# Keys times values in three strips of 32 columns instead of one block of 96

## The chip, the cores and the metric

The kernel runs on one core of a Trainium2 chip. The metric is the device time of one execution in microseconds (us). The core has five engines with their own instruction queues: TensorE (PE for its matmuls, PEld for its weight loads), VectorE (DVE), ScalarE (ACT), GpSimd (POOL) and SyncE (SP), which issues most of the DMAs.

## The reference

Three stages run one after the other: a gated linear attention with a complex decay, a dense gated layer, and a layer of eight experts of which each token visits one.

```python
for t in range(S):                        # batch 4, heads H = 8, S = 768, D = 48
    S_re, S_im = ar*S_re - ai*S_im + kv[t], ar*S_im + ai*S_re    # kv = outer(k[t], v[t])
    y[t] = q[t] @ S_re                                     # a_re, a_im normalised to |a| <= 0.999
x = y as (3072 tokens, 384)
x = ((x @ w_a) * (x @ w_b)) @ w_out       # w_a, w_b: 384x1536, w_out: 1536x384
e = argmax(x @ w_gate); out = softmax weight of e * (relu(x @ w1[e]) @ w2[e])   # 8 experts, 384 -> 1024 -> 384
```

## The kernel before

The 3072 tokens are worked on in twelve blocks of 256 tokens (j), three to a batch entry, and each block in two chunks (c) of 128 tokens. For the attention, the recurrence is turned into matrix products within a chunk plus a state that is carried from chunk to chunk. A head has 48 complex key channels, held as 96 rows (48 real, 48 imaginary parts). VectorE, ScalarE and GpSimd prepare the decays and phases of a block (`pre`), and DMAs bring keys and queries into the layout `kT`, `qT` (96 rows, heads, tokens).

For a chunk TensorE then does, in the function `attn`:

- `sc` (line 1209): keys times queries, four heads at a time, 128x128 scores each; VectorE masks them into `sm`.
- `kn` (line 1218): transposes of the keys, 128 tokens by 96 channels for each head; ScalarE copies them into `KN` (line 1223, tile `kn`).
- `y` (line 1248): the outputs. The 384 output channels are 12 pieces of 32 columns, and four pieces are worked on side by side: each matmul has a stationary operand of 32 columns (of `v`, or of the state `T`) and writes one of the four strips of 32 PSUM partitions. The moving operands are 128 columns wide.
- `kv` (line 1267): keys times values for the state. For each of the 8 heads one matmul, the stationary operand `KN` of 128 tokens by 96 channels, the moving operand `v` of 128 tokens by 48 columns, the result 96x48. VectorE adds it to the state (line 1273 or 1275, tile `T`) and fades it.

The last chunk of a batch entry needs no state after it, so `kv` is called 20 times: 24 chunks less four. All these operands are plain float32. Each such matmul stands in the trace as two weight loads and two matmuls (two passes): 8 matmuls of `kv` are 16 records.

The dense layer of a block follows: `up` (line 852, tile `ab_p`, 128x256 moving; for the first block line 859, in plain float32), gating on ScalarE, VectorE and GpSimd (`g`, `gH`, `gL`, lines 869 to 880), and `down` (line 889, tile `o`, moving 128x392). These use float32 split into a high and a low part, one pass each. The logits lead to a routing step (`rk`, line 587, bf16), and the experts run at the end (lines 710 and 728).

The order on each engine is set before the kernel is built, by a planner: every step is given to it with an engine, an estimated weight, what it reads and writes, and the time at which it is due (`P.add`), and the planner lays the steps of all blocks down engine by engine. So attention steps of block j stand between `up` and `down` steps of block j-1. The weight of `kv` in that plan, 1.36, is the same before and after. TensorE works through its queue in that order.

Of the kernel before, what the change touches and what calls it, by code (L numbers as in the profile page):

```python
# [15 lines left out]
H, D, C, BT = 8, 48, 128, 256  # L16
# [393 lines left out]
def fast(tc, q, k, v, a_re, a_im, w_a, w_b, w_out, w_gate, w1, w2, out, dram, x2d):  # L410

    nc = tc.nc
# [3 lines left out]
    with ExitStack() as mctx, ExitStack() as ctx:  # L416
# [424 lines left out]
        xT, ld, PT, KN, pq, made = {}, {}, {}, {}, {}, {}  # L841
# [349 lines left out]
        def attn(j, t0, t1):  # L1191
# [7 lines left out]
            for c in range(2):  # L1199
# [64 lines left out]
                def kv(c=c, S=S):  # L1264
                    t = S["kv"] = p_sc.tile([96, H, D], F32, tag="sc", name="kv_p")
                    for h in range(H):
                        nc.tensor.matmul(out=t[:, h], lhsT=KN[j, c][:, h], rhs=ld["v", j, c][:, h, 0:D], start=True, stop=True)

                def sum_(c=c, S=S, first=first):
                    T = tpad[(2 * j + c) % 2]  # L1270
# [29 lines left out]
                if not last:  # L1300
                    add("PE", 1.36, kv, [("kn", 0), ("kn", 1), v_], [("kv_p", j, c)], take="sc")
                    add("DVE", on("DVE", 384), sum_, [("kv_p", j, c), T_] + qk, [To_], give=True, alone=False)
                    add("DVE", 0.01 if first else on("DVE", 384), fade, [To_] + qk, [To_])
# [52 lines left out]
        for j in range(1, NB):  # L1356
# [14 lines left out]
            t = P.add("PE", 0.2, count, r=["oh", "acc"], w=["rk_p"], at=at + 2, take="sc")  # L1371
# [6 lines left out]
            if j == NB - 1:  # L1378
                P.add("DVE", 0.5, spanned, r=[("span", i, n) for i in range(3 * NF) for n in range(2)], w=["fit"], at=lo + 46)
                t = P.add("PE", 0.06, counted, r=["acc"], w=["so_p"], at=lo + 24, take="sc")  # L1380
# [77 lines left out]
```

## Time and profile before

| what | value |
|---|---|
| median of 3 timed runs | 944.06 us (941.37 to 945.06) |
| the profiled execution | 935.16 us |
| span of the profiled execution | 933.3 us |
| mean granted TensorE clock in it | 0.991 |
| TensorE matmul / weight load busy | 93% / 90% of the span |
| VectorE / ScalarE / GpSimd busy | 65% / 48% / 31% |
| `kv`: matmul records | 320, mean 247 ns each, 30.1 us busy |

The durations of matmuls overlap, since a matmul is started while the one before is still on its way through the array, and the end that the profile gives is modelled. What a matmul costs in a row of matmuls is therefore read from the distance between two starts, never from the duration. A timeline row gives the start of the first of a run of like instructions, the time from that start to the end of the last, and their number; the start of one row less the start of the row before it is what the earlier row cost TensorE.

### The profile page before, as it was taken

How to read it: one execution, taken by the hardware profiler on the slowest of the kernel's cores; microseconds unless marked ns; L12 is line 12 of the kernel's file. 1: busy time of each engine (PE TensorE's matmuls, PEld its weight loads, DVE VectorE, ACT ScalarE, POOL GpSimd, SP SyncE). 2: the span in 40 equal slices, each digit the busy share in tenths (PEclk: the TensorE clock that was granted, in tenths of full speed). 3: DMA queues.
4: the chain of work that ended last, by engine and by line, in shares of the span. 5: the costliest groups of instructions: out<-in, count | busy, mean ns of one | idle time of the engine just before them, and what ended most of it. 6: DMA issues, size and time to landing. Idle time of an engine off the chain costs nothing. (4 is left out here: it accounts for less than half of the span.)

```text
span 933.3 us, 18743 instructions
## 1 busy us (share of the span) xinstructions
PE 871.8 (93%) x7308; PEld 840.8 (90%) x7308; DVE 606.6 (65%) x1261; ACT 446.4 (48%) x821; POOL 288.8 (31%) x285
## 2 busy tenths in 40 slices
PE   0399899999999999999999999999999999999993
PEld 0387789899999999999999999999999999999993
DVE  7799989978676768595949496435652644545530
ACT  6453566666557354554645453224532543434430
POOL 3100002153253334352334333222235451433211
PEclk9999999999999999999999999999999999999997
DMA  9394521531625452716272715112433643454501
GB/s 250 98 337 133 178 52 50 155 112 35 162 44 162 102 154 60 213 44 195 62 194 44 212 28 153 35 52 69 139 117 114 178 143 102 147 165 131 161 23 24
DMA packets 128895, 112.69 MB, mean 121 GB/s; under 512 B 36564, under 2 KB 123446, under 8 KB 128796
## 3 DMA queue, kind: packets, MB, share of 16 engines
q1 hardware_dynamic: 122620, 101.30, 38.4%
q0 software_dynamic: 6176, 10.08, 3.8%
q8 instruction: 60, 0.98, 0.5%
q14 instruction: 39, 0.32, 0.1%
HBM read 82.42 MB, written 10.56 MB: 100 GB/s over the span
## 5 line engine op out<-in xcount | busy, mean ns | idle before, releaser
L852 PE MATMUL ab_p<-xH,wa 128*128 128x256 f32 x792 | 168.3, 289 | 0.7 <-ACT xH L1259 0.7
L852 PE MATMUL ab_p<-xH,wb 128*128 128x256 f32 x792 | 162.6, 282 | 0.0
L880 POOL TENSOR_TENSOR gL<-g,gH 128x256 fp32r<-128x256 f32 x108 | 94.8, 878 | 218.6 <-ACT gH L876 206.0
L869 ACT COPY g<-ab_p 128x256 f32<-128x256 f32 x144 | 53.5, 372 | 190.9 <-PE ab_p L852 168.9
L889 PE MATMUL o<-wo,gH 128*128 128x392 f32 x528 | 139.7, 345 | 0.0
L852 PEld LDWEIGHTS ab_p<-xH,wa 128*128 128x128 f32 x792 | 131.4, 189 | 3.1 <-issue 2.1
L852 PEld LDWEIGHTS ab_p<-xH,wb 128*128 128x128 f32 x792 | 131.7, 190 | 0.0
L872 DVE TENSOR_TENSOR g<-g,ab_p 128x256 f32<-128x256 f32 x144 | 59.9, 416 | 104.6 <-ACT g L869 104.4
L852 PE MATMUL ab_p<-xL,wa 128*128 128x256 f32 x396 | 111.5, 282 | 1.2 <-DVE xL L1262 1.2
L852 PE MATMUL ab_p<-xL,wb 128*128 128x256 f32 x396 | 111.6, 282 | 0.0
L715 DVE SCALAR_TENSOR_TENSOR hL<-h_p,hH 128x256 fp32r<-128x256 f32 (+5 forms) x80 | 41.4, 517 | 90.9 <-ACT hH L714 90.6
L714 ACT ACTIVATE hH<-h_p 128x256 fp32r<-128x256 f32 (+5 forms) x80 | 36.8, 460 | 111.7 <-PE h_p L710 110.8
L889 PE MATMUL o<-wo,gL 128*128 128x392 f32 x264 | 90.1, 341 | 0.0
L889 PEld LDWEIGHTS o<-wo,gH 128*128 128x128 f32 x528 | 89.2, 189 | 0.6 <-issue 0.4
L728 PE MATMUL o<-w2H,hH 128*128 128x384 f32 (+4 forms) x232 | 79.0, 341 | 0.0
L728 PE MATMUL o<-w2H,hL 128*128 128x384 f32 (+4 forms) x232 | 78.4, 338 | 0.0
L728 PE MATMUL o<-w2L,hH 128*128 128x384 f32 (+4 forms) x232 | 78.3, 337 | 0.0
L710 PE MATMUL h_p<-sH,w1H 128*128 128x256 f32 (+5 forms) x240 | 77.4, 322 | 0.0
L710 PE MATMUL h_p<-sH,w1L 128*128 128x256 f32 (+5 forms) x240 | 76.9, 320 | 0.0
L710 PE MATMUL h_p<-sL,w1H 128*128 128x256 f32 (+5 forms) x240 | 76.8, 320 | 0.0
L852 PEld LDWEIGHTS ab_p<-xL,wa 128*128 128x128 f32 x396 | 75.1, 190 | 1.8 <-DVE xL L1262 1.6
L876 ACT ACTIVATE gH<-g 128x256 fp32r<-128x256 f32 x132 | 54.6, 413 | 44.2 <-DVE g L872 44.0
(193 smaller groups left out, 1943.8 us busy)
## 6 DMA issues: line engine op xcount, KB each, us to landing
raw<-in_moe_w_dram SPq DMA_DIRECT2D x64, 384.0 KB, 3.8
q<-in_q_dram SPq DMA_DIRECT2D x24, 192.0 KB, 4.3
v<-in_v_dram SPq DMA_DIRECT2D x24, 192.0 KB, 3.7
raw<-in_moe_w_a_dram SPq DMA_DIRECT2D x12, 384.0 KB, 6.2
raw<-in_moe_w_b_dram SPq DMA_DIRECT2D x12, 384.0 KB, 6.7
raw<-in_moe_w_out_dram SPq DMA_DIRECT2D x12, 384.0 KB, 7.1
x2d<-x SPq DMA_DIRECT2D x24, 192.0 KB, 2.2
ck<-in_moe_w_a_dram SPq DMA_DIRECT2D x12, 384.0 KB, 3.7
```

The costliest lines, as they stand in the source:

```text
L710: nc.tensor.matmul(out=t, lhsT=lh[:, o:o + 128], rhs=rh[:, kk].rearrange("p c t -> p (c t)"), start=n == 0, stop=n == 8)
L714: nc.scalar.activation(out=hH, in_=t, func=ACTF.Relu)
L715: nc.vector.scalar_tensor_tensor(out=hL, in0=t, scalar=0.0, in1=hH.bitcast(F32), op0=ALU.max, op1=ALU.subtract)
L728: nc.tensor.matmul(out=G["o", c], lhsT=lh[:, c * r:(c + 1) * r], rhs=rh, start=f == 0 and n == 0, stop=f == NH - 1 and n == 2)
L852: nc.tensor.matmul(out=t[:, i], lhsT=lh[:, kk * 128:(kk + 1) * 128], rhs=rh[:, kk], start=n == 0, stop=n == 8)
L869: nc.scalar.copy(out=G["g", j, f], in_=G["ab", j, f][:, 0])
L872: nc.vector.tensor_tensor(out=G["g", j, f], in0=G["g", j, f], in1=G["ab", j, f][:, 1], op=ALU.mult)
L876: nc.scalar.activation(out=G["H", j, f], in_=G["g", j, f], func=ACTF.Copy)
L880: eng.tensor_tensor(out=G["L", j, f], in0=G["g", j, f], in1=G["H", j, f].bitcast(F32), op=ALU.subtract)
L889: nc.tensor.matmul(out=G["o", j, c], lhsT=lh[:, c * C:(c + 1) * C], rhs=rh, start=f == first and n == 0, stop=f == last and n == 2)
```

## The change

The loop over heads in `kv` gets an inner loop: instead of one matmul with 96 stationary columns, three matmuls with 32 stationary columns each, which write partitions 0 to 31, 32 to 63 and 64 to 95 of the same PSUM tile. The moving operand, 48 columns of `v`, is the same for the three.

```diff
                 def kv(c=c, S=S):
                     t = S["kv"] = p_sc.tile([96, H, D], F32, tag="sc", name="kv_p")
                     for h in range(H):
-                        nc.tensor.matmul(out=t[:, h], lhsT=KN[j, c][:, h], rhs=ld["v", j, c][:, h, 0:D], start=True, stop=True)
+                        for s in range(3):
+                            nc.tensor.matmul(out=t[s * 32:s * 32 + 32, h], lhsT=KN[j, c][:, h, s * 32:s * 32 + 32], rhs=ld["v", j, c][:, h, 0:D], start=True, stop=True)
```

No other instruction changes and none changes its place, on any engine. On TensorE each of the 20 rows of `kv` is replaced where it stands. Two kinds of place matter. In the first `kv` stands right behind `y`, whose stationary operands have 32 columns too; this is the difference of before and after on TensorE at the second call (a row is line, operation, tile written and operands, output partitions x columns, and count; the numbers are buffer numbers):

```order
 L1248 MATMUL y_p<-sm,v_131 32x128 x4
 L1248 MATMUL y_p<-qT,T_133 32x128 x4
-L1267 MATMUL kv_p<-v_131,kn 96x48 x8
+L1268 MATMUL kv_p<-v_131,kn 32x48 x24
 L803 MATMUL wt_p<-ident,raw 128x128 x3
 L859 MATMUL ab_p<-x,raw 128x256 x6
```

Eight matmuls have become 24, between the same neighbours. Seven of the 20 calls stand right behind `y`; one of the seven is followed by `rk`, the others by matmuls with 128 stationary columns. In the second kind of place `kv` stands between matmuls with 128 stationary columns. TensorE before, at one such call, in the middle of the kernel:

```order
L889 MATMUL o_4620<-wo_969,gL 128x392
L889 MATMUL o_4624<-wo_969,gH 128x392 x2
L889 MATMUL o_4624<-wo_969,gL 128x392
L1267 MATMUL kv_p<-v_130,kn 96x48 x8
L852 MATMUL ab_p<-xH,wa_1532 128x256
L852 MATMUL ab_p<-xL,wa_1532 128x256
```

and the same place after the change:

```order
L889 MATMUL o_4812<-wo_1001,gL 128x392
L889 MATMUL o_4816<-wo_1001,gH 128x392 x2
L889 MATMUL o_4816<-wo_1001,gL 128x392
L1268 MATMUL kv_p<-v_130,kn 32x48 x24
L852 MATMUL ab_p<-xH,wa_1596 128x256
L852 MATMUL ab_p<-xL,wa_1596 128x256
```

Only the row of `kv` differs (and buffer numbers). There are thirteen such calls: twelve behind `o` (eight with `ab` next, four with `rk` next) and the very first call, which stands behind `sc` and before `wt`.

## Rows read from the trace of the kernel before

**Rows 1.** The page: span, and busy time of the engines.
```profile
span 933.3 us, 18743 instructions
PE 871.8 (93%) x7308; PEld 840.8 (90%) x7308; DVE 606.6 (65%) x1261; ACT 446.4 (48%) x821; POOL 288.8 (31%) x285
```

**Rows 2.** Busy time by stage; columns as the first line names them.
```profile
core 0: us, PE busy (x) PEld busy (x) DVE busy (x) ACT busy (x) POOL busy (x), PEclk, DMA share, GB/s
60.00:110.00 50.00, 48.24 (x229) 39.04 (x229) 48.57 (x110) 21.77 (x46) 0.00 (x0) 1.00 0.70 217
110.00:130.00 20.00, 18.04 (x237) 16.32 (x236) 18.00 (x37) 15.02 (x28) 0.00 (x0) 0.91 0.17 41
...
260.00:420.00 160.00, 160.00 (x1590) 156.75 (x1590) 117.89 (x242) 86.17 (x155) 65.84 (x56) 1.00 0.42 113
420.00:610.00 190.00, 190.00 (x1828) 186.40 (x1826) 124.95 (x276) 87.31 (x166) 63.10 (x71) 1.00 0.43 114
```

**Rows 3.** Instructions of line 1267 (kv): count, ns min/median/max, first and last start.
```profile
L1267 PEld LDWEIGHTS kv_p<-v,kn x320: 159/165/165, 47.9 to 606.6; 128*96 128x96 f32 x160
L1267 PE MATMUL kv_p<-v,kn x320: 203/248/283, 48.1 to 606.7; 128*96 128x48 f32 x160
```

**Rows 4.** TensorE timeline, kv between o and ab: start, us, instructions.
```profile
308.31 0.34 PE L889 MATMUL o<-wo,gL 128*128 128x392 f32 x1
308.49 1.48 PE L1267 MATMUL kv_p<-v,kn 128*96 128x48 f32 x16
309.79 0.36 PE L852 MATMUL ab_p<-xH,wa 128*128 128x256 f32 x1
```

**Rows 5.** TensorE timeline, from ab into y, then kv and rk.
```profile
254.47 0.28 PE L852 MATMUL ab_p<-xL,wb 128*128 128x256 f32 x1
254.58 0.28 PE L852 MATMUL ab_p<-xH,wb 128*128 128x256 f32 x1
254.79 0.43 PE L1248 MATMUL y_p<-sm,v 128*32 128x128 f32 x8
255.03 0.41 PE L1248 MATMUL y_p<-qT,T 96*32 96x128 f32 x8
...
256.14 0.40 PE L1248 MATMUL y_p<-sm,v 128*32 128x128 f32 x8
256.36 0.40 PE L1248 MATMUL y_p<-qT,T 96*32 96x128 f32 x8
256.69 1.56 PE L1267 MATMUL kv_p<-v,kn 128*96 128x48 f32 x16
258.09 0.17 PE L587 MATMUL rk_p<-oh,strict 128*128 128x8 bf16 x1
258.12 0.17 PE L587 MATMUL rk_p<-acc,ones 128*128 128x8 bf16 x1
258.14 0.17 PE L587 MATMUL rk_p<-oh,strict 128*128 128x8 bf16 x1
```

**Rows 6.** TensorE timeline, from y out to ab.
```profile
322.95 0.40 PE L1248 MATMUL y_p<-qT,T 96*32 96x128 f32 x8
323.28 0.39 PE L852 MATMUL ab_p<-xH,wa 128*128 128x256 f32 x1
323.50 0.28 PE L852 MATMUL ab_p<-xL,wa 128*128 128x256 f32 x1
323.62 0.40 PE L852 MATMUL ab_p<-xH,wa 128*128 128x256 f32 x2
```

**Rows 7.** TensorE timeline, from y out to rk.
```profile
601.66 0.40 PE L1248 MATMUL y_p<-qT,T 96*32 96x128 f32 x8
602.00 0.18 PE L587 MATMUL rk_p<-oh,strict 128*128 128x8 bf16 x1
602.04 0.17 PE L587 MATMUL rk_p<-acc,ones 128*128 128x8 bf16 x1
```

**Rows 8.** TensorE timeline, a run of plain float32 matmuls with 256 moving columns.
```profile
57.04 2.76 PE L859 MATMUL ab_p<-x,raw 128*128 128x256 f32 x12
59.63 0.28 PE L812 MATMUL wg_p<-wg,wt 128*128 128x8 f32 x2
```

**Rows 9.** Weight loads that started in the first 70 ns of a y.
```profile
53.33 0.16 PEld L1248 LDWEIGHTS y_p<-sm,v 128*32 128x32 f32 x8
```

**Rows 10.** Records of kv by stage; columns us, PE busy (x), PEld busy (x), clock, DMA.
```profile
40.00:60.00 20.00, 3.04 (x32) 2.90 (x32) 1.00 0.89 270
110.00:130.00 20.00, 3.12 (x32) 2.87 (x32) 0.91 0.17 41
172.00:215.00 43.00, 1.56 (x16) 1.43 (x16) 0.96 0.40 114
215.00:260.00 45.00, 4.67 (x48) 4.30 (x48) 1.00 0.35 90
260.00:420.00 160.00, 7.39 (x80) 7.56 (x80) 1.00 0.42 113
420.00:610.00 190.00, 10.35 (x112) 10.59 (x112) 1.00 0.43 114
```

**Rows 11.** What TensorE waited for: us in total, times, longest.
```profile
PE kn_p L1218 <- DVE sm L1213: 1.7, 1, 1.7
PE ab_p L852 <- DVE xL L1262: 1.2, 2, 0.9
PE rk_p L587 <- DVE oh L565: 0.5, 1, 0.5
```

## The prediction

> **What bounds the kernel now.** I read the page first for the busy shares: TensorE has matmuls in flight for 93% of the span, VectorE is at 65%, the others below [rows 1]. Then the busy time by stage, since a share over the whole span says little: from 260 to 610 us TensorE is busy for every microsecond of 350, VectorE for 243 [rows 2]. There the end moves with what TensorE is given to do. From 60 to 110 us VectorE is busy 48.57 of 50 us, so time saved on TensorE ahead of that stretch would mostly be spent waiting. Third, what TensorE waits for: apart from the start-up there are a few waits, one of 1.7 us for VectorE's masks and small ones for `xL` and the routing [rows 11]. Last the timeline, for what a piece of work costs from start to start.
>
> The 20 calls of `kv` stand in the trace as 320 passes [rows 3]. By stage there are two calls before 60 us, two from 110 to 130, one from 172 to 215, then 3, 5 and 7, which makes 15 after 215 us [rows 10].
>
> **What kv costs now.** Between `o` and `ab` it takes 309.79 - 308.49 = 1.30 us, 81 ns a pass [rows 4]. Is that the moving operand? Plain float32 with 256 moving columns takes (59.63 - 57.04) / 12 = 216 ns a pass [rows 8], so 48 columns would be 40 ns in proportion. So a pass of `kv` waits for the load of its 96 stationary columns, about 0.85 ns a column; 32 columns then take about 27 ns. Behind `y` the call takes 258.09 - 256.69 = 1.40 us [rows 5].
>
> **What a strip costs.** The trace shows an operation of this kind: `y` has 32 stationary columns and writes four strips in turn. Eight of its passes start every 0.22 us [rows 5], which is two rounds of four strips at 0.11 us a round. One strip's 128 moving columns alone take half of 216, 108 ns. So the four strips run at the same time, and the load of the next 32 columns (27 ns) is hidden under the matmul. Loads of different strips also run together: the first eight passes of `y` take 255.03 - 254.79 = 0.24 us instead of 0.22, one load of 27 ns for all and not four in turn; and eight weight loads start within 70 ns of its beginning [rows 9].
>
> By this, the new `kv` is 16 rounds (8 heads, two passes) of three strips side by side, each round as long as 48 moving columns. That lies between 40 ns (in proportion) and 44 ns (110 less 80 columns at 0.83 ns, the slope between y's 110 and 216). I take 44, for y's rounds hold the overheads that these will: 16 x 44 = 0.70 us. The bounds of a round are 27 ns from below (a load alone, if the matmul were hidden under it) and 81 to 85 ns from above (three loads of 27 ns one after another, and a few ns between them); I keep to the row of `y`, the only one of this kind.
>
> **What turning the array over costs.** Going into strips and out of them isn't free, and `y` shows both. In: the last `ab` before `y` takes 254.79 - 254.58 = 0.21 us where its neighbour takes 0.11, so 0.10, and 0.02 for the slower first rounds. Out: y's last eight start at 322.95, `ab` at 323.28, 0.33 instead of 0.22, and the first `ab` takes 0.22 where the next takes 0.12, since its weights are not loaded ahead: 0.11 + 0.10 [rows 6]. With `rk` behind it, 602.00 - 601.66 = 0.34 and then 0.04 instead of about 0.03: 0.12 + 0.01 [rows 7]. So there and back costs 0.33 us, or 0.25 with `rk` next. Before the change a `kv` behind `y` paid the way out itself (256.69 - 256.36 = 0.33); it now follows in place at 0.22 and pays the way out at its own end.
>
> **The sum on TensorE.**
> - behind `o` or `sc`, `ab` or `wt` next, 9 calls: 1.30 - (0.70 + 0.33) = 0.27 us each, 2.4
> - behind `o`, `rk` next, 4 calls: 1.30 - (0.70 + 0.25) = 0.35, 1.4
> - behind `y`, six calls: (0.33 + 1.40) - (0.22 + 0.70 + 0.21) = 0.60, 3.6
> - behind `y`, `rk` next, one call: 1.73 - (0.22 + 0.70 + 0.13) = 0.68, 0.7
>
> Together 8.1 us. The 15 calls after 215 us (8 of the first kind, 4, 2 and 1) hold 2.2 + 1.4 + 1.2 + 0.7 = 5.5, and there TensorE has no idle time that could swallow it. The first two calls (0.9) stand ahead of the stretch in which VectorE is full: I count nothing. The three between 110 and 215 us hold 1.8; TensorE waits for masks, `xL` and the routing near them [rows 11], so half, 0.9. That makes 6.4 us, between 4.5 (some of the rest meets waits too) and 8.1. The profiled execution took 935.16 us and would take 928.8. The timed runs had a median of 944.06, 9 us above it; I take the same 6.4 us off and forecast 937.6 us, faster by 0.7%.
>
> What else the edit touches: a call issues 16 more matmuls, 32 more passes, whose issue is inside the rounds (the first rival prices it if it isn't). The order on the other engines stays, so nothing is moved past a queue and no wait is added. VectorE's sum waits for the last pass of `kv` and gets it earlier.
>
> **A rule against it.** Passes of `y` average 27.5 ns apart, and nothing in a long row in this trace is denser; `rk` with 8 moving columns has 20 to 30 ns between starts [rows 5]. The Trainium skill, TensorE: Matmul & The Clock Gate, section "Wait — 56ns, not 53.3ns?", says that starts of matmuls are never nearer than about 25 ns, however few columns move. By that rule 48 passes would take 48 x 25 = 1.20 us and the change would lose. In the trace eight loads and their first matmuls start within 70 ns [rows 9], so it is no limit between strips in a burst; whether it is one on the average, no row shows, since y's rounds would be 110 ns anyway.
>
> The same page (section "The mechanism") lets a weight load overlap a matmul in flight only if they use different rows of the array. All strips here use all rows, so a round would be 27 + 44 = 71 ns. The trace speaks against it: y's rounds take 110 ns with 108 of moving, so loads were hidden there.
>
> **Rivals.** The gain of 8.1 us is spread over 20 x 16 = 320 rounds, 25 ns each: the change breaks even on TensorE at about 69 ns a round. All rivals on TensorE are told by that number.
>
> - *Issue bounds it* (13%). If passes can't start nearer than 25 to 27.5 ns on the average, a round is 75 to 82 ns, 31 to 38 above mine. In the 15 late calls that is 240 rounds: 5.5 - 7.4 to 5.5 - 9.1, so 2 to 4 us lost: 946 to 948. For it: nothing denser in a row. Against it: the bursts in `y`.
> - *Strips take turns* (10%), the slower side. If the three loads go one after the other the round is 85 ns: 5.5 - 240 x 0.041, 4.3 us lost, 948. If the matmuls take turns too, 48 passes of 44 ns, a round is 131 ns: 5.5 - 240 x 0.087 = 15 us lost and 3 more in the early calls: 962. Loads that are not hidden (71 ns) would end near no change, 945. For it: three strips that read the same moving columns at once occur nowhere in the trace. It decides from 69 ns a round on. Against it: y's 0.24 and 0.22 us.
> - *TensorE gains and another engine takes it back* (15%). Then the `kv` rows shorten as forecast, but `up` or `down` waits for gating or masks; 0 to 4 us gained, 942. For it: VectorE is at 74% from 260 to 420 us. Against it: TensorE has no idle time there at all, so the others are ahead by more than the few tenths that a call saves.
>
> The forecast case holds the other 62%, with a range of its own from 934 to 940.5.
>
> **How the numbers follow.** A measurement of this kernel can tell about 0.5%, 4.7 us, from no change. The forecast's 6.4 us lies not far beyond that: of its 62%, 47 count as faster and 15 as no change. The issue case is mostly within 0.5% (10, and 3 slower), taking turns mostly slower (8, and 2 within), the third within (15). That makes faster 0.47, same 0.42, slower 0.11. The range reaches down to 933 (rounds somewhat shorter and the early calls counted), and up to 947 to take in the third case and most of the issue case.
>
> **What would show it.** In the new profile `kv` stands as 960 passes. Right: from its first start to that of the `ab` behind it about 1.03 us where it was 1.30; behind `y` it starts 0.22 us after y's last eight and not 0.33; the first `ab` or `o` behind it is slower by 0.10; the last `ab` or `o` ahead of it as well; TensorE still busy throughout 260 to 610 us, and the stretch of the dense blocks shorter by 5 to 6 us. Wrong: a `kv` of 1.2 us or more inside (issue or turns), new waits of TensorE for `g`, `sm` or `xL` (the third case), or a lower granted clock in the stretches around the calls.

## The result and the profile after

The changed kernel took 934.37 us (median of four runs, 931.75 to 935.85), the kernel before 944.56 us in the same set: a ratio of 0.9904, 95% interval 0.9881 to 0.9927. That ratio is worth 9.1 us. In a second set, with more runs, it was 927.78 against 935.83 us, 0.9912 (0.9894 to 0.9930), which is 8.2 us by the ratio. Forecast were 6.4 us, 0.9932.

There are two profiles of the changed kernel, from these two sets. Where the lines agree the second is shown. First the page, span and busy time of the engines, which answer to [rows 1]:

```profile
span 925.7 us, 20023 instructions
PE 862.1 (93%) x7948; PEld 827.8 (89%) x7948; DVE 605.8 (65%) x1261; ACT 446.1 (48%) x821; POOL 293.6 (32%) x285
```

TensorE has 640 records more of each kind and is busy for less time; its share of the span has not moved. The instructions of line 1268, which is the new `kv` [rows 3]:

```profile
L1268 PEld LDWEIGHTS kv_p<-v,kn x960: 106/110/112, 49.2 to 599.4; 128*32 128x32 f32 x192
L1268 PE MATMUL kv_p<-v,kn x960: 203/206/231, 49.2 to 599.4; 128*32 128x48 f32 x192
```

320 passes have become 960, and the last starts at 599.4 us instead of 606.7. Busy time by stage, columns as in [rows 2]:

```profile
260.00:420.00 160.00, 160.00 (x1802) 154.87 (x1801) 119.42 (x244) 85.41 (x155) 64.53 (x57) 1.00 0.43 115
420.00:610.00 190.00, 190.00 (x2037) 184.54 (x2036) 124.96 (x282) 88.06 (x167) 64.99 (x72) 1.00 0.42 111
```

TensorE is still busy for all of the 350 us, at the full clock, so what it was spared there has reached the end. The call between `o` and `ab`, the same as in [rows 4], on the timeline of TensorE:

```profile
305.31 0.34 PE L889 MATMUL o<-wo,gH 128*128 128x392 f32 x1
305.49 0.34 PE L889 MATMUL o<-wo,gL 128*128 128x392 f32 x1
305.76 0.88 PE L1268 MATMUL kv_p<-v,kn 128*32 128x48 f32 x48
306.57 0.38 PE L852 MATMUL ab_p<-xH,wa 128*128 128x256 f32 x1
306.80 0.28 PE L852 MATMUL ab_p<-xL,wa 128*128 128x256 f32 x1
```

From its own first start to that of the next instruction `kv` takes 0.81 us where it took 1.30. The `o` ahead of it takes 0.27 instead of 0.18: the way into strips. The `ab` behind it takes 0.23, since its weights are not loaded ahead. And a call behind `y` with `rk` next, the one of [rows 5]:

```profile
254.54 0.40 PE L1248 MATMUL y_p<-qT,T 96*32 96x128 f32 x8
254.76 0.86 PE L1268 MATMUL kv_p<-v,kn 128*32 128x48 f32 x48
255.55 0.18 PE L587 MATMUL rk_p<-oh,strict 128*128 128x8 bf16 x1
255.59 0.17 PE L587 MATMUL rk_p<-acc,ones 128*128 128x8 bf16 x1
```

It starts 0.22 us after y's last eight passes instead of 0.33, and takes 0.79 where it took 1.40.

The first of the two profiles shows something else. Its span is 932.9 us, hardly below the 933.3 before. There the first matmul of the experts stands 7.7 us earlier than before, and TensorE is 7.7 us ahead still at 700 us; then, on its timeline:

```profile
701.95 0.28 PE L710 MATMUL h_p<-sL,w1H 128*128 128x256 f32 x1
702.06 0.28 PE L710 MATMUL h_p<-sH,w1L 128*128 128x256 f32 x1
705.60 0.39 PE L710 MATMUL h_p<-sH,w1H 128*128 128x256 f32 x1 [3.26 <-issue]
```

It stood still for more than 3 us with nothing named that it waited for. By stage (columns as in [rows 2]):

```profile
700.00:705.00 5.00, 2.34 (x20) 2.14 (x18) 0.62 (x1) 0.88 (x2) 3.90 (x4) 1.00 0.38 103
705.00:710.00 5.00, 3.66 (x16) 3.16 (x16) 0.85 (x2) 0.47 (x2) 3.91 (x4) 0.65 0.14 36
```

VectorE and ScalarE do little, and after the pause the granted clock falls to 0.65 on the mean, part of the time at the lower level. By 715 us all 7.7 us are gone. Read against the first profile of the kernel before, which had no such pause, the change would seem to bring 0.4 us of span. The first experiments ask whether this belongs to the change.

### The profile page after: what moved, and what is told of

The parts are those of the page before. It is cut to its first block, busy times and chain, and to the rows that moved or that the text cites. A ratio compares the mean times of both kernels' runs of the same rounds, so it can differ in the third digit from the quotient of the medians.

```text
span 932.9 us, 20023 instructions
## 1 busy us (share of the span) xinstructions
PE 865.6 (93%) x7948; PEld 829.9 (89%) x7948; DVE 606.7 (65%) x1261; ACT 446.6 (48%) x821; POOL 288.5 (31%) x285
```

## The experiments

Theory: three strips run side by side, a round is as long as its moving columns, going into strips and out costs a fixed turn, and TensorE hands the saved time on because it has no idle time. Rivals: the issue of passes or the loads bound a round; the late pause belongs to the strips and eats the gain; the time comes from somewhere else.

### Both kernels again

The kernel before, unchanged.

> The kernel before, unchanged, with a second profile of its own. In the first pair of profiles the changed kernel was 7.7 us ahead at 607 us and 0.4 us ahead at the end, since TensorE stood still around 702 us in the dense run of the experts; the timed runs say 9 us in all. Theory A (stalls of that kind come and go between executions in both kernels): this execution is at or above 941 us and shows idle TensorE or a lower clock after 660 us that the first profile of before did not show; up to 607 us it agrees with that profile within 0.5 us. Theory B (the strips cause the late stall): no such stall here, about 935 us in the profile.

It took 935.93 us (ratio to itself in the set 1.0003, 0.9989 to 1.0017) and showed no pause. What theory A forecast for this run, 941 us or more and an idle TensorE, did not come: the pause is not shown in the kernel before, and theory A stands on the next run alone.

The changed kernel, unchanged.

> The changed kernel, unchanged, with a second profile. Both theories: the last kv stands 7.5 to 8 us earlier than in the kernel before. Theory A: no stall at 702 us this time, or one at another place, with 930 to 935 us and a ratio of 0.988 to 0.993. Theory B: the same stall of 3.5 us at the same place again.

927.78 us, ratio 0.9912, and no pause: from 700 to 800 us

```profile
700.00:800.00 100.00, 100.00 (x616) 96.82 (x615) 48.20 (x75) 40.80 (x75) 47.98 (x42) 1.00 0.47 138
```

TensorE is busy throughout. The weight loads of the experts (count, ns, first and last start), in the kernel before of the same set and in this run:

```profile
L710 PEld LDWEIGHTS h_p<-sH,w1H x240: 186/188/193, 671.8 to 908.3; 128*128 128x128 f32 x120
L710 PEld LDWEIGHTS h_p<-sH,w1H x240: 186/188/193, 664.4 to 900.8; 128*128 128x128 f32 x120
```

The first is 7.4 us ahead, the last 7.5. So the changed kernel is 7.4 us ahead before the experts start, the experts keep it, and theory B falls as it was put (the same pause at the same place again): none of the six profiles of kernels with strips in this second round of runs has such a pause among the experts. That strips bring one now and then is not ruled out by one profile with a pause and six without. Nor do the times settle it: both kernels took longer in the first set than in the second (8.7 and 6.6 us by the medians), and the first profile of the kernel before, 935.16 us, lies below all four timed runs of that set; whether pauses stood in those runs no profile shows. What the pause was stays open. What counts for reading is that the end of one profile can hide a gain that the same profile shows at every earlier mark.

### Another order of the same matmuls

```diff
-                    for h in range(H):
-                        for s in range(3):
+                    for s in range(3):
+                        for h in range(H):
```

> The same 24 matmuls a call in another order: the strip is the outer loop and the head the inner one, so that eight matmuls of one strip stand behind one another in the queue before the next strip comes. If strips run side by side only when neighbours in the queue use different strips, a call takes about 48 x 44 ns = 2.1 us instead of 0.70, and the kernel is 20 x 1.4 = 28 us slower than the changed one, some 20 us slower than before. Rival (each strip has a queue of its own that looks far ahead): a call stays near 0.7 to 1.0 us and the time within 3 us of the changed kernel.

945.57 us, ratio 1.0104 (1.0082 to 1.0126): slower than before, 17.8 us slower than the changed kernel. The same kind of call on the timeline:

```profile
310.49 0.34 PE L889 MATMUL o<-wo,gL 128*128 128x392 f32 x1
310.76 1.95 PE L1268 MATMUL kv_p<-v,kn 128*32 128x48 f32 x48
312.64 0.38 PE L852 MATMUL ab_p<-xH,wa 128*128 128x256 f32 x1
```

1.88 us against 0.81 for the same 48 passes. How many passes were in flight in 0.2 us at the beginning of a call (line 1268; columns us, PE busy (x), PEld busy (x), clock, DMA), strip by strip first:

```profile
310.80:311.00 0.20, 0.20 (x5) 0.20 (x6) 1.00 0.00 0
311.00:311.20 0.20, 0.20 (x9) 0.20 (x7) 1.00 0.11 3
```

and in the changed kernel:

```profile
305.80:306.00 0.20, 0.20 (x16) 0.20 (x18) 1.00 0.00 0
306.00:306.20 0.20, 0.20 (x28) 0.20 (x21) 1.00 0.11 3
```

Three times as many. So neighbours in the queue must use different strips. The call is still somewhat shorter than 48 passes one by one (48 x 42 ns is 2.0 us, and the way out comes on top). The single starts in the trace lie 42 or 43 ns apart, except for a few shorter distances (6 to 37 ns) around each of the two changes of strip. That fits a TensorE that begins the next strip while a few passes of the old one are still to come; the records don't name the strip, so this reading is not shown. My 28 us were too many for that (1.07 us a call, not 1.4), and because the early calls are partly hidden: the fifteen calls after 215 us cost 15.9 us against the changed kernel, the five ahead of it 0.8.

### What bounds a round

Strips with 64 moving columns, of which 16 are padding that nothing reads (the tile for the result is made wider to hold them):

```diff
-                            nc.tensor.matmul(out=t[s * 32:s * 32 + 32, h], ..., rhs=ld["v", j, c][:, h, 0:D], start=True, stop=True)
+                            nc.tensor.matmul(out=t[s * 32:s * 32 + 32, h], ..., rhs=ld["v", j, c][:, h], start=True, stop=True)
```

> Three strips as in the changed kernel, but 64 moving columns instead of 48: the 16 padding columns of v behind each head move too, and what they give is not read. If the moving columns set the length of a round (about 0.83 ns a column, and 42 ns at 48), a round takes 56 ns and 16 rounds 0.22 us more a call; if the issue of passes sets it, a round stays at 42 ns.

```profile
308.12 1.09 PE L1269 MATMUL kv_p<-v,kn 128*32 128x64 f32 x48
309.14 0.39 PE L852 MATMUL ab_p<-xH,wa 128*128 128x256 f32 x1
```

1.02 us against 0.81, 0.21 more: 13 ns a round for 16 columns, 0.83 ns a column (rounds of 42.5 and 55.8 ns by the single starts). The one execution took 931.66 us. The moving columns set the round.

The kernel before with 64 moving columns:

> The kernel before with 64 moving columns instead of 48, 96 stationary columns as they were. If a pass of kv waited for the load of its weights there, the pass stays at 81 to 85 ns and the call at 1.30 us; if it waited for the moving columns, it grows by a third.

```profile
308.60 1.49 PE L1268 MATMUL kv_p<-v,kn 128*96 128x64 f32 x16
309.90 0.36 PE L852 MATMUL ab_p<-xH,wa 128*128 128x256 f32 x1
```

1.30 us, as with 48 columns, and 935.36 us in the one execution. A third more to move costs nothing there: the pass waited for the load of its 96 columns.

The 48 columns in two halves, each with loads of its own:

```diff
                     for h in range(H):
-                        for s in range(3):
-                            nc.tensor.matmul(out=t[s * 32:s * 32 + 32, h], ..., rhs=ld["v", j, c][:, h, 0:D], start=True, stop=True)
+                        for d in range(0, D, 24):
+                            for s in range(3):
+                                nc.tensor.matmul(out=t[s * 32:s * 32 + 32, h, d:d + 24], ..., rhs=ld["v", j, c][:, h, d:d + 24], start=True, stop=True)
```

> Three strips, and the 48 moving columns in two halves of 24, each with its own weight loads: 48 matmuls and 96 passes a call, 32 rounds. A round is then no longer bounded by the moving columns (20 ns). Loads side by side would bound it at 27 to 30 ns, 0.9 to 1.0 us for the 32 rounds; an issue limit of 25 ns between any two passes, the first rival of the prediction, would make 75 ns a round and 2.4 us a call.

```profile
313.18 1.21 PE L1269 MATMUL kv_p<-v,kn 128*32 128x24 f32 x96
314.32 0.38 PE L852 MATMUL ab_p<-xH,wa 128*128 128x256 f32 x1
```

96 passes in 1.14 us, of which 0.12 lie between the last start and the `ab` (single starts in the trace): 1.02 us over 32 rounds is 32 ns a round and 11 ns a pass. That rules out 25 ns between starts on the average, and three loads one after another (81 ns a round). The kernel as a whole took 938.04 us in the one execution. Against the second profile of the kernel before it was 3.3 us behind at 130 us, 4.3 at 265 and 3.5 at 615: what it lost it lost ahead of 265 us, and the late calls won 0.8 back. Within two calls TensorE waited for nothing the profile names:

```profile
PE kv_p L1269 <- issue: 2.6, 2, 2.1
58.78 0.28 PE L1269 MATMUL kv_p<-v,kn 128*32 128x24 f32 x8 [2.10 <-issue]
262.54 0.18 PE L1269 MATMUL kv_p<-v,kn 128*32 128x24 f32 x1 [0.54 <-issue]
```

The first line gives the total in us, the times and the longest; the other two, from the timeline, the places. Why it waited there wasn't tried.

### The price of the turn

`kv` joined to `y` in the plan, so that it always stands right behind it. Its own step goes, its weight in the plan falls from 1.36 to 0.8, and `y` now waits for `kn` too, so the planner may order other steps anew (operands that stay are cut to `...`):

```diff
-                add("PE", 1.0 if first else 1.9, y, [("sm", 0), ...] + qk, ["y"])
+                y_r = [("sm", 0), ...] + qk
+                if last:
+                    add("PE", 1.0 if first else 1.9, y, y_r, ["y"])
+                else:
+                    add("PE", 0.8 + (1.0 if first else 1.9), lambda y=y, kv=kv: (y(), kv()), y_r + [("kn", 0), ("kn", 1)], ["y", ("kv_p", j, c)], take="sc")
 ...
-                    add("PE", 1.36, kv, [("kn", 0), ("kn", 1), v_], [("kv_p", j, c)], take="sc")
```

> Strips kept, and kv always given to the planner as one step with y, so that it stands right behind y in all 20 calls and not in 7. If the turn into strips and back costs 0.33 us (0.25 with rk next), 13 calls save one turn each: 4.0 us less than the changed kernel up to 607 us, ratio to the kernel before about 0.987. Rival (a turn is cheap, the shorter kv comes from the rounds alone): no difference from the changed kernel beyond 1 us.

923.20 us, ratio 0.9856 (0.9835 to 0.9877), 4.6 us below the changed kernel. In place it looks like this:

```profile
303.49 0.40 PE L1248 MATMUL y_p<-qT,T 96*32 96x128 f32 x8
303.71 0.86 PE L1268 MATMUL kv_p<-v,kn 128*32 128x48 f32 x48
304.51 0.18 PE L587 MATMUL rk_p<-oh,strict 128*128 128x8 bf16 x1
```

0.22 us after `y`, no turn. The profiled execution was the longest of its four (925.80 us): the first expert load stands at 662.6 us, 1.8 us ahead of the changed kernel; but between 185 and 615 us alone it gained 4.1 us on it (the same matmuls of `up`, counted through, 2.4 us behind at the first mark and 1.7 ahead at the second), 3.7 of them after 265 us. It had fallen behind early, by 4.4 us at 140 us: from 110 to 130 us the plan came out in another order and TensorE's granted clock was 0.83 on the mean (1.00 in the second profile of the changed kernel), part of the time at the lower level:

```profile
110.00:130.00 20.00, 17.62 (x294) 16.08 (x292) 15.20 (x33) 14.26 (x27) 0.00 (x0) 0.83 0.11 22
```

So the two were parted: joined from block 4 on only.

```diff
+                joined = not last and j >= 4
```

> Strips, and kv joined to y in the plan from block 4 on; the first seven calls are planned as in the changed kernel. With kv joined everywhere the plan of the stretch around 110 to 133 us came out worse (TensorE 4.9 us late there and about 2.4 us lost for good against the changed kernel), while the twelve late calls gained 4.1 us. If both parts are rightly read, this version keeps the 4.0 us of the late turns and loses nothing early: 4 us less than the changed kernel, ratio to the kernel before 0.986 to 0.988, and in the trace 4 us ahead of the changed kernel at the last up of the dense layer. Rival (the gain of the joined kernel came from a better order elsewhere): no more than 1.5 us below the changed kernel.

922.21 us, ratio 0.9868 (0.9850 to 0.9885) in a later set; the first expert load stands at 659.0 us, 5.4 us ahead of the changed kernel's second profile and 12.8 ahead of that of the kernel before. About 3.5 us of the 5.4 come after 265 us, where the late turns are. Of the rest 1.4 us come from 185 to 190 us, and not from the plan: the same 54 matmuls of `up` stand there in the same order, but the granted clock was 0.72 in the changed kernel and 1.00 here (changed kernel first, columns as in [rows 2]):

```profile
185.00:190.00 5.00, 5.00 (x34) 5.00 (x34) 3.63 (x6) 0.84 (x3) 1.89 (x2) 0.72 0.02 4
185.00:190.00 5.00, 5.00 (x45) 5.00 (x44) 4.67 (x9) 1.58 (x4) 2.67 (x3) 1.00 0.01 0
```

The two joined kernels can't be told apart by their times. Both beat the changed kernel (0.9912), and the price of a turn is as read from `y`: 12 late calls, 3.6 us by the prediction's 0.33 and 0.25, 3.7 and 3.5 measured from 265 to 615 us, where the clock was full in all three.

## Why the prediction was right, and what it mis-sized

- *What bounds the kernel.* Right. From 260 to 610 us TensorE has no idle time before or after, and 4.76 us of the gain arise there, all of it handed on. The same matmuls of `up` stand 2.97 us earlier than before at 268 us and 7.73 earlier at 607; the lead grows in twelve steps of 0.36 to 0.43 us, one at each call, and no other step exceeds 0.03, so the time comes from `kv` and its neighbours and not from elsewhere.
- *A pass before waits for its load.* Shown: with 64 moving columns it stays as it was.
- *Three strips side by side, a round of 44 ns.* Shown. It is 42: the last pass of a call starts 0.14 us ahead of the `ab` (single starts in the trace), and 0.81 less 0.14 is 0.67 for 16 rounds, the first of 66 ns and the others of 42 to 43. The moving columns set it, the order of the queue is needed for it.
- *The turn.* Right in place and size, shown by the joined kernels. (The sign "about 1.03 us" for the call itself counted the whole turn into it; by the terms of the sum it is 0.70 + 0.02 + 0.11 = 0.83, and 0.81 was measured.) But one term of the sum was mis-sized: behind `o` I charged the new `kv` 0.10 us for the slow first `ab` and overlooked that the old `kv` made its `ab` slow as well. It stands in the trace of before, one row below [rows 4]:

```profile
309.79 0.36 PE L852 MATMUL ab_p<-xH,wa 128*128 128x256 f32 x1
309.99 0.28 PE L852 MATMUL ab_p<-xL,wa 128*128 128x256 f32 x1
```

  0.20 us, where an `ab` among its like takes 0.12: an estimate fits, by which 128 columns at 0.85 ns take 109 ns to load and a pass of 48 moving columns covers 40 of them. So 0.08 of the 0.10 had been paid already. From the `o` ahead to the second `ab` the call took 1.68 us (308.31 to 309.99) and now takes 1.31: 0.37 saved and not 0.27. Of the fifteen late calls ten have an `ab` or `o` behind them, which makes 0.8 us; the calls themselves came out 0.02 to 0.03 us shorter than reckoned, another 0.4. Together the fifteen gained 6.7 to 6.8 us instead of 5.5, the twelve behind `o` 4.7 to 4.8 of it instead of 3.6. This is the difference between the 6.4 us of the forecast and the 7.4 to 7.7 at the start of the experts.
- *The early calls.* The number was about right, in part by luck. Calls one to eight gained 3.0 us in one pair of profiles and 2.8 in the other, where I counted 2.8; the five ahead of 215 us gave 1.0 and 0.8 of it, where I counted 0.9. But these 0.9 were half of a sum, a guess, and the traces do not show that the five calls earned them. In the first pair the lead is 0.1 us still at 110 us, as forecast, and 1.6 at 123: in between, TensorE's granted clock was lower in the kernel before (its first profile, then the second profile of the changed kernel, which agrees with the first here):

```profile
115.00:120.00 5.00, 5.00 (x84) 4.62 (x77) 3.59 (x9) 3.57 (x7) 0.00 (x0) 0.76 0.00 0
115.00:120.00 5.00, 4.76 (x118) 4.43 (x110) 4.97 (x11) 4.61 (x9) 0.00 (x0) 1.00 0.21 43
```

  In the second pair the clock was full in both from 110 to 130 us, and the lead is 1.8 us from 58 us through to 200; the second profile of the kernel before ran 1.8 us later than its first there, without any change. Ahead of 215 us two executions of one kernel thus differ by more than the gain in question.
- *Rivals.* Issue and taking turns are ruled out by the 32 ns rounds; in the strip-by-strip kernel the strips do take turns, and it is slower than before, by 9.7 us. No other engine took the gain back after 215 us. Ahead of it some was: TensorE's waits in the second profile of the changed kernel (us in total, times, longest), two that the kernel before didn't have:

```profile
PE sc_p L1209 <- DMA kT<-k: 0.8, 1, 0.8
...
PE y_p L1248 <- DVE sm L1213: 0.6, 1, 0.6
```

- *The two rules of the Trainium skill.* TensorE: Matmul & The Clock Gate, section "Wait — 56ns, not 53.3ns?", gives about 25 ns as the least distance of two starts; across strips the runs here show 11 ns on the average. Section "The mechanism" of that page of the Trainium skill lets a load overlap only if the rows differ; here loads under all 128 rows were hidden behind matmuls in other strips and in their own, since a round of 42 ns has no room for a load of 27 and 40 of moving columns one after the other.
- *The size in the timed runs*, 8.2 us with an interval from 6.6 to 9.9, holds the 7.4 to 7.7 of the traces. The 9 of the first set are within its interval.

## What to carry to other kernels

A plain float32 matmul with few moving columns (48 and 64 here, under 96 columns of weights) waits for its weights; cut into strips of 32 columns that alternate in the queue, loads and matmuls of all strips run together and the moving columns set the pace (not with 24, where a round took 32 ns and the columns alone would take 20). Each excursion into strips and back cost about 0.3 us here, so put such work next to other strip work, or don't do it for less than that. And read what a neighbour pays today before charging a change for it.

## What the runs showed of the hardware beyond that

- Between strips, passes with a weight load each started 11 ns apart on the average over 96 passes (24 moving columns, plain float32), with rounds of 32 ns; neighbouring strips started 6 or 7 ns apart.
- The order of the queue decides: the same 48 passes took 0.67 us alternating and about 1.74 us strip by strip, without the way out. Shorter distances than 42 ns between starts stand only around the two changes of strip, a few at each.
- One execution of the changed kernel paused for more than 3 us among the experts with no engine busy that it waited for, after which the granted clock was below full for some microseconds. No other profile here shows it, and its cause is open.
- The same kernel, executed twice, can differ by 1.8 us in the middle: the second profile of the kernel before ran that much later than the first from 58 to 110 us, and 0.3 later from 140 us on. From 115 to 120 us the granted clock was 0.76 on the mean in the first and 1.00 in the second.
